# Splitting the late output-projection weights around the last keys and values, and moving the last group's transposes together

## The chip, the cores and the metric

The kernel runs on one core of a Trainium2 chip. The core has a matrix engine (PE, whose weight loads the profile lists as PEld), a vector engine (DVE), a scalar engine (ACT), a general engine (POOL) and SyncE (SP), which here issues all transfers. The metric is the device time of one execution in microseconds; smaller is better.

## The reference

One decoding step (one new token for each of four sequences) of a block: attention over a cached window and a gated feed-forward part, both modulated by a condition c. All data are 32-bit floats.

```python
mod = (silu(c) @ w_mod).reshape(4, 6, 1, 512)         # sa, ca, ga, sb, cb, gb
h = layernorm(x) * (1 + ca) + sa                       # x: 4 x 1 x 512
q = (h @ wq)                                           # 32 heads of 128
k, v = last 2048 rows of k_cache, v_cache              # 8 key heads, each shared by 4 query heads
a = softmax(q k^T / sqrt(128)) v @ wo                  # wo: 4096 x 512
x = x + ga * a
h = layernorm(x) * (1 + cb) + sb
x = x + gb * ((silu(h @ w1) * (h @ w3)) @ w2)          # w1, w3: 512 x 1792; w2: 1792 x 512
```

## The kernel before

**Memory and transfers.** Some 101 MB are read once, in the order in which they are used. They pass through one buffer, `ring`, of three slots; a slot has two halves of 8192 floats a partition. `load(dst, src, cuts)` issues on SP one transfer for each piece that `cuts` names. SP issues in program order, and an issue waits until the piece's old content has been used. The order is: modulation weights of the first part, x and c, wq, then the keys and values (K and V) of the eight groups of heads, 8 MB a group, in turn into the slots. Group g's load is written behind group g-3. Group 7's load is written behind group 5, in two pieces (K, then V) into slot 1. Ahead of it in the queue goes `wo_mod` into slot 0: the first half of wo (for groups 0 to 3) with the modulation weights of the second part. Behind group 7's go the second half of wo (4 MB, for groups 4 to 7) into the place of group 6's K, `w1` into that of group 6's V, then `w3` in two pieces and `w2` in five (6, 4, 2, 1 and 1 of its 14 chunks) into slot 0.

**A group (`group(g)`, line 310).** Scores: four tiles `s_ps[t]` of 512 keys each, four products (one for each sequence) into a tile, and a maximum `mx` on DVE. Then `heads_out(g - 1)` (line 303) turns the previous group's result `o_sb` into columns of `oT` with four products and a DVE copy. Then for each tile t: an exponential on ACT into `p_sb[t]`, four transposes on PE into one of two PSUM banks that alternate, a DVE copy to `pT[t]`, and, one tile behind, the products with V, which add up in `o_ps` over the four tiles. Last, ACT scales `o_ps` into `o_sb`.

**The projection (`project_out(g)`, line 294).** Four products of `oT[:, g]` with wo, added up in `a_ps` over the eight groups. Those of groups 0 to 3, and the modulation's columns `mod_b`, stand between groups 6 and 7 on PE; those of groups 4 to 6 stand behind group 7; then come `heads_out(7)` and the projection of group 7.

**The rest.** Lines 358 to 403 follow one upon another: copy of `a_ps`, a norm and modulation (`norm`, `modulate`, `transposed`, short steps on PE, DVE and ACT), `ffn_in` with w1 and with w3 (16 products each, over the four parts k of 512 in turn, then transposes), the 14 chunks of products with w2, two DVE operations and the store.

Each float product is shown in the profile as two MATMUL instructions, so a projection is 8 of them and a group's scores are 32. All operations are recorded through one helper, so that all have line 53 in the profile; tiles tell them apart. Waits are derived from the buffers that operations touch: the part of a load's target that is overwritten decides what SP waits for.

Of the kernel before, what the change touches and what calls it, by code (L numbers as in the profile page):

```python
# [8 lines left out]
B, D, HQ, G, SK, DH, W, FF = 4, 512, 32, 8, 8192, 128, 2048, 1792  # L9
P = 128  # L10
R = HQ // G
NT = 4
# [6 lines left out]
HALF = 8192  # L19
# [122 lines left out]
def block_kernel(nc, xc_in, w_mod_a, wq, kv_in, wo_mod, wo, w1, w3, w2, out):  # L142
# [5 lines left out]
    do = Program(nc)  # L148

    def sb(name, *shape):  # L150
        return nc.alloc_sbuf_tensor(name, (P, *shape), F32).ap()

    def ps(name):
        return nc.alloc_psum_tensor(name, (P, 512), F32).ap()

    ring = sb("ring", 6 * HALF)
    slots = [ring[:, n * 2 * HALF : (n + 1) * 2 * HALF] for n in range(3)]
    s_ps = [ps(f"s_ps{t}") for t in range(NT)]
    banks = [ps(f"bank{n}") for n in range(2)]
    a_ps, o_ps = ps("a_ps"), ps("o_ps")  # L160
    turn = [0]

    def bank():
        turn[0] += 1
        return banks[turn[0] % 2]

    def load(dst, src, cuts=(0, 1)):
        step = src.shape[1] // cuts[-1]
        for lo, hi in zip(cuts[:-1], cuts[1:]):
            do("sync", "dma_start", dst[:, lo * step : hi * step], src[:, lo * step : hi * step])  # L170
        return dst[:, : src.shape[1]]
# [13 lines left out]
    kv = [None] * G  # L185
# [28 lines left out]
    oT = sb("oT", G, R, B)  # L214
# [9 lines left out]
    ss, ln, r0, ve, a, r = (sb(n, 1) for n in ("ss", "ln", "r0", "ve", "a", "r"))  # L224
# [68 lines left out]

    def project_out(g):
        for i in range(R):
            do("tensor", "matmul", a_ps[32 * i : 32 * i + B, :], oT[:, g, i, :], wo_t[g // 4][:, g % 4, i, :], start=(g == 0), stop=(g == G - 1))

    mx, nm, ls, l, rl = (sb(n, m) for n, m in (("mx", NT), ("nm", 1), ("ls", NT), ("l", 1), ("rl", 1)))
    p_sb = [sb(f"p_sb{t}", 512) for t in range(NT)]
# [3 lines left out]
    def heads_out(g):  # L303

        otp = bank()[:, : R * B]
        for c in range(NC):
            do("tensor", "matmul", otp, o_sb[:, c * P : (c + 1) * P], pick[:, c].rearrange("p r b -> p (r b)"), start=(c == 0), stop=(c == NC - 1))
        do("vector", "tensor_copy", oT[:, g].rearrange("p r b -> p (r b)"), otp)

    def group(g):  # L310
        kt, vt = (kv[g][:, i * HALF : (i + 1) * HALF].rearrange("p (t b n) -> p t b n", t=NT, b=B) for i in range(2))
        for t in range(NT):
            for b in range(B):
                do("tensor", "matmul", s_ps[t][32 * b : 32 * b + 32, :], qT[:, g, b, :], kt[:, t, b, :], start=True, stop=True)
            do("vector", "reduce_max", mx[:, t : t + 1], s_ps[t], axis=AX.X)
        do("vector", "tensor_reduce", nm, mx, axis=AX.X, op=ALU.max, negate=True)
        if g:
            heads_out(g - 1)
        for t in range(NT):
            do("scalar", "activation", p_sb[t], s_ps[t], AF.Exp, bias=nm, accum_out=ls[:, t : t + 1])  # L320
            pt = bank()
            for c in range(NC):
                do("tensor", "transpose", pt[:, c * P : (c + 1) * P], p_sb[t][:, c * P : (c + 1) * P], ident)
            do("vector", "tensor_copy", pT[t], pt.rearrange("p (c b i) -> p b c i", b=B, i=32)[:, :, :, :R])
            for u in [t - 1] * (t > 0) + [t] * (t == NT - 1):
                for b in range(B):
                    do("tensor", "matmul", o_ps[32 * b : 32 * b + NC * R, :], pT[u][:, b].rearrange("p c r -> p (c r)"), vt[:, u, b, :], start=(u == 0), stop=(u == NT - 1))
        do("vector", "reduce_sum", l, ls, axis=AX.X)
        do("vector", "reciprocal", rl, l)
        do("scalar", "activation", o_sb, o_ps, AF.Copy, scale=rl)  # L330

    for g in range(G - 1):
        group(g)
        if g < 4:
            kv[g + 3] = load(slots[(g + 2) % 3], kv_in[g + 3])
        elif g == 4:
            wom = load(slots[0], wo_mod)
        elif g == 5:
            load(slots[1], kv_in[7], (0, 1, 2))
            kv[7] = slots[1]  # L340
    wo_t = [t.rearrange("p (g r n) -> p g r n", g=4, r=R) for t in (wom[:, :HALF], load(slots[2][:, :HALF], wo))]
    w1_t = load(slots[2][:, HALF:], w1)
    for g in range(4):
        project_out(g)
# [2 lines left out]
    ga, sh, cb1, gb = (mod_b[:, i * P : (i + 1) * P] for i in range(4))  # L347
    mod_columns(wom[:, HALF:].rearrange("p (k j i) -> p k j i", k=4, j=4), mod_b, 4)
    do("vector", "tensor_scalar_add", cb1, cb1, 1.0)
    group(G - 1)  # L350
    w3_t = load(slots[0][:, HALF:], w3, W3_CUTS)
    w2_t = load(slots[0][:, :HALF], w2, W2_CUTS)
    for g in range(4, G - 1):
        project_out(g)
    heads_out(G - 1)
    project_out(G - 1)

    do("scalar", "copy", work, a_ps)
# [49 lines left out]
def _layout(i):  # L408
    import numpy as np

    def a(t):
        return np.ascontiguousarray(t)

    k = i["A_k_cache"][:, :, SK - W :, :].reshape(B, G, NT, 512, DH)
    v = i["A_v_cache"][:, :, SK - W :, :].reshape(B, G, NT, NC, P, DH)
    wm = i["w_mod"].reshape(4, P, 6, 4, P)
    xc = np.zeros((4, 32, P + 16), np.float32)
    xc[:, ::8, :P] = i["A_x"].reshape(B, 4, P).transpose(1, 0, 2)
    xc = xc.reshape(P, P + 16)
    xc[:, P:] = i["c"].reshape(B, 4, P).transpose(2, 1, 0).reshape(P, 16)  # L420
    w2 = i["B_w2"].reshape(14, P, D)
    wo = a(i["A_wo"].reshape(2, 4, R, P, D).transpose(0, 3, 1, 2, 4)).reshape(2, P, 8192)
    return {
        "xc_in": xc,
        "w_mod_a": a(wm[:, :, :2].transpose(1, 0, 3, 2, 4)).reshape(P, 4096),
        "wq": a(i["A_wq"].reshape(4, P, G, 512).transpose(1, 2, 0, 3)).reshape(P, 16384),
        "kv_in": np.concatenate([k.transpose(1, 4, 2, 0, 3).reshape(G, P, 8192), v.transpose(1, 4, 2, 0, 3, 5).reshape(G, P, 8192)], 2),
        "wo_mod": np.concatenate([wo[0], a(wm[:, :, 2:].transpose(1, 0, 3, 2, 4)).reshape(P, 8192)], 1),
        "wo": wo[1],
        "w1": a(i["B_w1"].reshape(4, P, FF).transpose(1, 0, 2)).reshape(P, 4 * FF),  # L430
        "w3": a(i["B_w3"].reshape(4, P, FF).transpose(1, 0, 2)).reshape(P, 4 * FF),
        "w2": a(np.stack([w2[4 * j + c] for c, j in CHUNKS], 1)).reshape(P, NF * D),
    }
# [15 lines left out]
```

## Time and profile before

| | |
|---|---|
| Median of 3 runs | 244.43 us (244.31 to 244.51) |
| The profiled execution's own time | 243.92 us |
| Its span, first to last instruction | 242.5 us |
| Mean granted clock of PE | 0.866 of full speed |
| Read from memory | 101.26 MB, 418 GB/s over the span |
| Busy: PE, DVE, ACT, POOL | 147.2, 47.6, 33.4, 2.1 us |

A row of the timeline has the start and the length in us, the engine, the operation with what it writes and reads, the count of instructions merged into the row, and in brackets how long the engine had stood idle and what ended that. In the chain of waits each entry is a start, a length and what the time was spent in, each released by the one before it. In the rows of stretches, "PE busy (x)" is busy time with the number of instructions, and PEclk the granted clock. The load of q1 is the DMA queue that SP feeds.

### The profile page before, as it was taken

Reading aid. Unit: us, or ns where it says so; the run is one execution under the profiler, and the core shown is the slowest. Engines: PE = TensorE matmul, PEld = TensorE weight load, DVE = VectorE, ACT = ScalarE, POOL = GpSimd, SP = SyncE. Lnnn points to the kernel's source line nnn. Section 1 sums busy time; section 2 is a strip of 40 time slices with the busy share of each in tenths; the row PEclk is TensorE's granted clock in tenths of the full one; section 3 lists DMA queues with packets and bytes.
Section 4 is the critical chain, followed back from the end, with each engine's and each line's share of the span. In section 5 each row is a group of like instructions: output and inputs, shape, how many; then the busy total and the mean of one; then the engine's idle time right before and its main releaser. Section 6 shows DMA issues by size and latency. Waiting matters only on the chain.

```text
span 242.5 us, 2543 instructions
## 1 busy us (share of the span) xinstructions
PE 147.2 (61%) x1106; PEld 52.2 (22%) x1106; DVE 47.6 (20%) x155; ACT 33.4 (14%) x84; POOL 2.1 (1%) x9
## 2 busy tenths in 40 slices
PE   0260392088278558838819919838836885873975
PEld 0120121023014113204202302411411232121234
DVE  3230003042023014104105103203200150104021
ACT  2000000004104103103200310410410022101020
POOL 3000000000000000000000000000000000000000
PEclk9999999579859958979967985997995996798599
DMA  7997979898989898989898999999999999999992
GB/s 251 453 519 346 519 346 511 357 508 358 497 368 489 378 497 368 489 378 486 378 486 381 476 390 476 411 446 411 454 405 405 430 432 432 432 435 407 426 410 95
DMA packets 3322, 101.48 MB, mean 418 GB/s; under 512 B 368, under 2 KB 624, under 8 KB 1008
## 3 DMA queue, kind: packets, MB, share of 16 engines
q1 hardware_dynamic: 3312, 101.33, 97.4%
q8 instruction: 8, 0.13, 0.2%
q14 instruction: 2, 0.02, 0.0%
HBM read 101.26 MB, written 0.07 MB: 418 GB/s over the span
## 4 chain that ended last, share of the span: by engine, by line
DMA 74%; PE 21%; DVE 2%; ACT 1%; issue 1%; SPq 1%; DVEq 0%; ACTq 0%
DMA ring<-kv_in 56%; DMA ring<-wo 18%; PE s_ps L53 12%; PE bank L53 4%; PE o_ps L53 3%; PE a_ps L53 2%; ACT p_sb L53 1%; SPq L53 1%; DVE mx L53 0%; DVE sq L53 0%; DVE p_sb L53 0%; ACT work L53 0%; DVE h L53 0%; DVE x L53 0%; DVE xc L53 0%
## 5 line engine op out<-in xcount | busy, mean ns | idle before, releaser
L53 PE MATMUL s_ps<-ring,qT 128*32 128x512 f32 x256 | 43.0, 833 | 43.0 <-DMA ring<-kv_in 43.0
L53 DVE TENSOR_REDUCE mx<-s_ps 128x1 f32<-128x512 f32 x32 | 22.1, 692 | 75.6 <-PE s_ps L53 75.6
L53 ACT ACTIVATE p_sb<-s_ps,nm 128x512 f32<-128x512 f32 x32 | 21.6, 686 | 104.8 <-PE bank L53 88.0
L53 PE MATMUL o_ps<-ring,pT 128*16 128x512 f32 x256 | 33.8, 624 | 2.9 <-DMA ring<-kv_in 2.9
L53 PE MATMUL bank<-ident,p_sb 128*128 128x128 f32 (+1 forms) x136 | 22.6, 290 | 10.4 <-ACT p_sb L53 9.8
L53 PEld LDWEIGHTS s_ps<-ring,qT 128*32 128x32 f32 x256 | 9.8, 148 | 75.5 <-DMA ring<-kv_in 39.5
L53 PEld LDWEIGHTS bank<-ident,p_sb 128*128 128x128 f32 (+1 forms) x136 | 14.7, 144 | 30.8 <-ACT p_sb L53 14.9
L53 DVE COPY pT<-bank 128x64 f32<-128x64 f32 x32 | 7.2, 225 | 42.0 <-PE bank L53 42.0
L53 PE MATMUL s_ps<-ring,hT 128*32 128x512 f32 x64 | 8.5, 693 | 10.5 <-DMA ring<-wq 10.5
L53 PE MATMUL a_ps<-ring,oT 128*4 128x512 f32 x64 | 9.4, 730 | 8.5 <-DMA ring<-wo_mod 6.0
L53 ACT ACTIVATE o_sb<-o_ps,rl 128x512 f32<-128x512 f32 x8 | 5.5, 687 | 41.1 <-PE o_ps L53 41.1
L53 PE MATMUL s_ps<-ring,h2T 128*32 128x512 f32 (+1 forms) x64 | 9.8, 705 | 0.4 <-DVE h2T L53 0.4
L53 PEld LDWEIGHTS bank<-pick,o_sb 128*128 128x128 f32 x64 | 7.8, 191 | 6.8 <-issue 6.8
L53 PE MATMUL bank<-pick,o_sb 128*128 128x16 f32 x64 | 8.5, 265 | 0.0
L53 PEld LDWEIGHTS o_ps<-ring,pT 128*16 128x16 f32 x256 | 5.1, 96 | 12.1 <-issue 9.6
L53 PE MATMUL bank<-tot,avg 128*128 128x1 f32 x4 | 1.0, 311 | 10.8 <-DVE tot L53 10.1
L53 PE MATMUL bank<-ring,sc 128*32 128x256 f32 (+1 forms) x64 | 7.2, 612 | 0.0
L53 ACT ACTIVATION_READ_ACCUMULATOR p_sb<-s_ps,nm 128x1 f32 x32 | 6.5, 203 | 0.0
L53 DVE COPY qT<-bank 128x64 f32<-128x64 f32 x8 | 2.2, 276 | 19.6 <-PE bank L53 19.3
L53 PEld LDWEIGHTS s_ps<-ring,hT 128*32 128x32 f32 x64 | 2.4, 127 | 16.0 <-issue 16.0
L53 PEld LDWEIGHTS a_ps<-ring,oT 128*4 128x4 f32 x64 | 1.6, 96 | 15.5 <-DMA ring<-wo_mod 6.9
L53 ACT ACTIVATE work<-s_ps 128x512 f32<-128x512 f32 x2 | 1.2, 597 | 24.4 <-PE s_ps L53 21.0
(72 smaller groups left out, 42.8 us busy)
## 6 DMA issues: line engine op xcount, KB each, us to landing
ring<-kv_in SPq DMA_DIRECT2D x2, 4096.0 KB, 42.8
ring<-wo SPq DMA_DIRECT2D x1, 4096.0 KB, 43.2
ring<-w SPq DMA_DIRECT2D x1, 3584.0 KB, 43.6
ring<-w SPq DMA_DIRECT2D x2, 1792.0 KB, 35.8
ring<-w_mod_a SPq DMA_DIRECT2D x1, 2048.0 KB, 7.9
ring<-w SPq DMA_DIRECT2D x1, 1536.0 KB, 40.4
ring<-w SPq DMA_DIRECT2D x1, 1024.0 KB, 42.4
ring<-w SPq DMA_DIRECT2D x1, 512.0 KB, 43.2
```

The source lines that it names most:

```text
L53: op = Op(engine, lambda: getattr(getattr(self.nc, engine), method)(*args, **kw), [])
```

## The change

The second half of wo is loaded as two quarters of 2 MB, into the same place as before. The third quarter (groups 4 and 5) is issued ahead of the last K, the fourth (groups 6 and 7) behind the last V and ahead of w1. The issue of the last K and V is now written behind group 6, behind the third quarter's. `wo_t` becomes a list of eight pieces, one for each group. In group 7 the projections of groups 4 and 5 stand between `heads_out(6)` and the transposes; all four tiles' transposes stand ahead of the first product with V; and the projection of group 6 stands behind `heads_out(7)`.

```diff
 def project_out(g):
     for i in range(R):
-        do("tensor", "matmul", a_ps[32 * i : 32 * i + B, :], oT[:, g, i, :], wo_t[g // 4][:, g % 4, i, :], start=(g == 0), stop=(g == G - 1))
+        do("tensor", "matmul", a_ps[32 * i : 32 * i + B, :], oT[:, g, i, :], wo_t[g][:, i, :], start=(g == 0), stop=(g == G - 1))
...
-def group(g):
+def group(g, projected=()):
...
     if g:
         heads_out(g - 1)
+    for done in projected:
+        project_out(done)
     for t in range(NT):
...
-        for u in [t - 1] * (t > 0) + [t] * (t == NT - 1):
+        if g < G - 1:
+            ready = range(max(t - 1, 0), t if t < NT - 1 else NT)
+        else:
+            ready = range(NT) if t == NT - 1 else ()
+        for u in ready:
             for b in range(B):
                 do("tensor", "matmul", o_ps[...], pT[u][...], vt[:, u, b, :], ...)
...
-    elif g == 5:
-        load(slots[1], kv_in[7], (0, 1, 2))
-        kv[7] = slots[1]
-wo_t = [t.rearrange("p (g r n) -> p g r n", g=4, r=R) for t in (wom[:, :HALF], load(slots[2][:, :HALF], wo))]
+quarters = [load(slots[2][:, : HALF // 2], wo[0])]
+kv[7] = load(slots[1], kv_in[7], (0, 1, 2))
+quarters.append(load(slots[2][:, HALF // 2 : HALF], wo[1]))
+wo_t = [t[:, n * 2048 : (n + 1) * 2048].rearrange("p (r n) -> p r n", r=R) for t in (wom[:, : HALF // 2], wom[:, HALF // 2 : HALF], *quarters) for n in range(2)]
 w1_t = load(slots[2][:, HALF:], w1)
...
-group(G - 1)
+group(G - 1, [4, 5])
 w3_t = load(slots[0][:, HALF:], w3, W3_CUTS)
 w2_t = load(slots[0][:, :HALF], w2, W2_CUTS)
-for g in range(4, G - 1):
-    project_out(g)
 heads_out(G - 1)
+project_out(G - 2)
 project_out(G - 1)
...
-        "wo": wo[1],
+        "wo": a(wo[1].reshape(P, 2, 4096).transpose(1, 0, 2)),
```

## The prediction

> **What bounds the kernel now.** I read the page first, for what is full over the whole span.
>
> ```profile
> span 242.5 us, 2543 instructions
> ...
> q1 hardware_dynamic: 3312, 101.33, 97.4%
> ```
>
> One queue fed by SP carries 101.33 MB and keeps its 16 engines busy for 97.4% of 242.5 us. The change moves the same bytes, so only what follows the stream can change. That is in the last entries of the chain of waits (start, length, what):
>
> ```profile
> 170.01 43.25 DMA ring<-wo
> ...
> 213.31 2.76 PE a_ps L53 x24
> ...
> 217.32 1.09 PE a_ps L53 x8
> ...
> 224.12 6.26 PE s_ps L53 x20
> ...
> 231.66 3.64 PE s_ps L53 x20
> ...
> 236.93 3.31 PE s_ps L53 x112
> ```
>
> The end does not hang on the last transfer. It hangs on wo, landed at 213.26: projections of groups 4 to 6 (24 matmul instructions), group 7's heads, its projection (8), the norm, the w1 products at 224.12, the w3 products at 231.66 and the w2 products at 236.93, without a wait for a transfer after wo. The question is how far behind this chain the stream is. The next fence pairs SP's issues (start) with their times to landing (last column), for w1, for the second half of w3 and for the last piece of w2, and gives the first and last start of the 112 w2 matmuls:
>
> ```profile
> 178.22 15.88 SPq L53 DMA_DIRECT2D ring<-w  x4
> ring<-w SPq DMA_DIRECT2D x1, 3584.0 KB, 43.6
> 193.30 0.33 SPq L53 DMA_DIRECT2D ring<-w  x1
> ring<-w SPq DMA_DIRECT2D x1, 1792.0 KB, 37.1
> 195.57 7.38 SPq L53 DMA_DIRECT2D ring<-w  x1
> ring<-w SPq DMA_DIRECT2D x1, 256.0 KB, 43.5
> L53 PE MATMUL s_ps<-ring,hidT x112: 272/273/298, 236.9 to 239.9; 128*32 128x128 f32 x112
> ```
>
> w1 lands at 178.22 + 43.6 = 221.8, 2.3 us ahead of its first use; the second half of w3 at 230.4; the last chunk of w2 at 195.57 + 43.5 = 239.07. That chunk is matmuls 105 to 112: 104/111 of the 2.99 us from first to last start puts it at 239.73. So the stream is only 239.73 - 239.07 - 0.05 (landing to first matmul, as 213.26 to 213.31) = 0.61 us ahead of the chain. This is the ceiling of the change: however much the chain gains, behind the last landing come 242.5 - 239.73 = 2.77 us of last chunk, two DVE operations and the store.
>
> **The change part by part.** The terms come from the timeline (start, length, instruction, idle time before it) of groups 6 and 7:
>
> ```profile
> 164.84 5.11 PE L53 MATMUL s_ps<-ring,qT 128*32 128x512 f32 x32 [4.86 <-DMA ring<-kv_in]
> 169.87 1.06 PE L53 MATMUL bank<-pick,o_sb 128*128 128x16 f32 x8
> 173.00 0.69 ACT L53 ACTIVATE p_sb<-s_ps,nm 128x512 f32<-128x512 f32 x1
> 175.70 0.66 PE L53 MATMUL bank<-ident,p_sb 128*128 128x128 f32 x4
> 184.18 5.65 PE L53 MATMUL a_ps<-ring,oT 128*4 128x512 f32 x32 [5.98 <-DMA ring<-wo_mod]
> 193.88 3.64 PE L53 MATMUL s_ps<-ring,qT 128*32 128x512 f32 x32 [0.62 <-DMA ring<-kv_in]
> 203.68 1.91 PE L53 MATMUL o_ps<-ring,pT 128*16 128x512 f32 x8 [2.90 <-DMA ring<-kv_in]
> 209.16 1.91 PE L53 MATMUL o_ps<-ring,pT 128*16 128x512 f32 x16
> 211.14 0.69 ACT L53 ACTIVATE o_sb<-o_ps,rl 128x512 f32<-128x512 f32 x1 [9.79 <-PE o_ps L53]
> ```
>
> *The queue.* The third quarter is issued once group 6's first two score tiles are done (half of 5.11 us behind 164.84, and late because the clock is low there: about 168.3), and the last K and V wait behind it on SP, though their own buffer is free earlier. At 168.3 wo_mod is still in flight and lands at 184.18, so 16 us of transfer cover the later issue; I cost it at nothing. If that cover were gone, each us would delay everything behind. One more DMA (0.33 us on SP) is likewise covered. SP's last issue already stalls for 7.38 us with no harm, since nothing stands behind it until the store; with one more transfer outstanding it may stall until V lands, 30 us ahead of its landing at 239.07. Costed at zero.
>
> *Landings.* Between the waits that wo_mod and K ended lie 9.70 us for 4 MB, so a 2 MB quarter takes 4.85. The third lands near 189.0, K at 198.7 instead of 193.85, V at 208.5 instead of 203.65, the fourth at 213.3, where wo landed. All behind it stays put. The rows of a quarter are half as long (16 KB). w3, whose two halves have rows of 14 KB, was complete 230.4 - 221.8 = 8.6 us behind w1: 2 x 1792 KB at 427 GB/s, against 432 for K, which on 4 MB is 0.1 us. I take 0.05, and 0 to 0.15 for the range.
>
> *The clock ahead of K.* PE finishes the modulation's columns at 193.88 - 0.62 = 193.26 and now idles 5.4 us until K. Here are windows of 3.41 us that begin where the granted clock changes (us, PE busy, clock, DMA share, GB/s):
>
> ```profile
> 161.01:164.42 3.41, 0.00 (x0) 1.00 0.99 423
> 164.42:167.84 3.42, 3.00 (x16) 0.50 1.06 460
> 167.84:171.25 3.41, 3.10 (x28) 1.00 0.84 365
> 198.56:201.97 3.41, 1.26 (x8) 1.00 1.05 452
> 201.97:205.38 3.41, 1.70 (x8) 0.50 0.98 423
> 205.38:208.80 3.42, 3.42 (x18) 0.50 0.98 417
> 208.80:212.21 3.41, 2.27 (x20) 1.00 0.99 426
> 222.45:225.86 3.41, 2.22 (x15) 0.50 0.97 412
> 225.86:229.28 3.42, 3.42 (x23) 0.50 1.04 440
> ```
>
> A full-clock window with 0.00 or 1.26 us of work is followed by half clock. A half-clock window with 3.00 or more is followed by full clock; one with 1.70 or 2.22 is not. With the same windows, 195.14 to 198.56 is empty, so the clock falls at 198.56, and the scores, from 198.75, fill the next window as group 6's did. They take group 6's 5.11 rather than 3.64, plus 0.1 for the slightly longer half-clock part: ended at 203.95. The Trainium skill, "TensorE: Matmul & The Clock Gate", Part 1, says that an idle window of about 3.4 us halves the clock and a busy one restores it; the trace agrees (0.50 behind the window of 0.00 us, 1.00 behind those of 3.00 and 3.42), and this rule speaks against the change here. Without the rule the sum would have scores of 3.64 us and PE 1.5 us earlier, which the ceiling makes worth nothing.
>
> *Group 7.* Heads of group 6 end 1.0 later, 204.95. Projections 4 and 5, 16 instructions, take 16/24 of the 2.76 us that 24 took behind wo, 1.8, to 206.75. The first exponentials are ready by then; the last ends as in group 6, 173.69 - 164.84 = 8.85 behind the scores' start, 207.6 (plus 0.1). So the projections put off the transposes by about 0.9 us. Four tiles at 0.66: ended at 209.4, behind V's landing at 208.5. The products with V then run without a break, 2 x 1.91 = 3.8, to 213.2 (211.07 before). Copy of the result 0.07 + 0.69, heads 1.0: 215.0. Projection 6 (0.9) covers the heads' copy to oT, projection 7 takes 1.04: ended at about 217.0 against 218.36. The chain gains 1.35 us: of the 2.76 us of projections behind wo 0.9 stay, and the later K and V take back the rest of the difference.
>
> *Behind it.* The w1 products can start at 224.12 - 1.35 = 222.75, still 0.95 behind w1's landing. They fill the window from 222.45 for 3.1 us, so the clock rises at 225.86 instead of 229.28: by group 6's rate (3.00 us at half clock do what 1.53 us at full clock do) they end near 227.9 instead of 230.4. The w3 products follow 1.28 later as before, at 229.2, and need w3's second half 1.8 us in, at 231.0; it landed at 230.4. The w2 products start 5.27 behind those, as 236.93 behind 231.66, at 234.5. They now run into the pieces of w2, and the last one starts at 239.07 + 0.05. Even if the clock rose as late as before, 6.5 us at half clock and 0.3 at full clock would end the w1 products at 229.6, 0.8 us earlier than before, and 0.61 is needed.
>
> *Sum.* Ceiling 0.61; less 0.05 for the shorter rows, and 0.02 of a possible 0.25 for a clock that falls while PE waits for pieces of w2 (the last chunk takes 0.5 us to DVE and half as much again at half clock, if one window of about 1.9 us of work counts as idle; 1.70 did not raise it and 1.26 dropped it, so this is undecided, though the drop would mostly come too late). Gain 0.54 us: span 241.96. The profiled execution took 243.92 us, 1.42 beside its span, and the shown median, 244.43, lies 0.5 above it. Taken off the median: 243.89.
>
> **The rivals.** *The stream ends no differently, and the chain gains nothing.* The phase of the windows decides. Group 5 met its keys 1.5 us into a window, which did not fill, and its scores took longer:
>
> ```profile
> 145.48 6.24 PE L53 MATMUL s_ps<-ring,qT 128*32 128x512 f32 x32 [5.42 <-DMA ring<-kv_in]
> ```
>
> With 6.24 for 5.11 the gain of 1.35 falls to 0.2, and with it the whole gain: 244.2. For it: PE idles ahead of K for 5.4 us, as ahead of group 5. Against it: the boundary at 198.56 lies 0.2 us ahead of K's landing. The Trainium skill ("TensorE: Matmul & The Clock Gate", Part 1) says that the windows run free of the kernel's start; the three runs, within 0.2 us, do not look like it.
>
> *Slower: the transposes behind the projections.* If the window with the scores does not restore the clock at all before 205.38, the scores take 6.9, and heads, projections, transposes and V products follow one upon another, with V long landed: 198.75 + 6.9 + 1.0 + 1.8 + 2.64 + 3.8 = 214.9, then 3.75 us to the end of projection 7, 218.7, which is 0.35 later than before. With the half-clock part of the w1 products unimproved, 244.8; a little more if heads or projections run at half clock too. It decides from 1.35 us of extra work at half clock between K and the last product. For it: every wait there is gone, so nothing absorbs a delay. Against: group 6's row.
>
> *Faster than the ceiling.* The runs shown are 0.5 us longer than the profiled one. If that is PE at half clock and not the stream, the same last landing cuts off up to 1.1: 243.3. Nothing in the profile tells.
>
> *The change does nothing since the stream bounds already.* The 0.61 is exact to about 0.1 in this execution; an end set by the stream in the other runs would leave 244.4.
>
> **How the numbers follow.** A difference of about 0.2%, 0.49 us, is what measurement of this kernel can tell. The end on the last piece of w2 has 0.58, with a range of its own of 243.65 to 244.1; some two thirds of it lie below 243.94. Below the ceiling 0.10; the chain or the stream giving nothing 0.14 and 0.05; slower 0.13. So faster 0.38 + 0.10 = 0.48, same 0.20 + 0.19 = 0.39, slower 0.13. The range, 243.3 to 244.7, takes in the extra of the shown runs and stops short of the slower rival's end.
>
> **What the profile after would show.** K's wait ends near 198.7 and V is no longer waited for; granted clock 0.50 from 198.6 to 202; projections 4 and 5 (16 instructions) behind the heads of group 6; projection 7 ended near 217.0; the w1 products start near 222.7; and the chain ends on a transfer of w2 (239.1), not on wo. A last w2 landing later than 239.3, scores above 6 us, or a projection 7 ended after 217.9 would make the prediction wrong.

## The result and the profile after

The changed kernel took 243.40 us (the median of six runs, from 243.22 to 243.73), the kernel before, beside it, 245.02 (six runs, 244.31 to 245.98): a ratio of 0.9934, with a 95% interval of 0.9906 to 0.9961. Measured once more the ratio was 0.9945 (0.9921 to 0.9970). The profiled executions took 243.22 us against 243.92. So the gain is 0.70 us between the two profiles and 1.0 to 1.6 us between the medians measured side by side; that difference is the main thing to explain. Part of it is sampling: the kernel before spreads so widely that its median is 245.02 over these six runs, 244.41, 244.37 and 244.21 over 33, 35 and 17 later ones, and 243.90 over 17 more.

The page has the same stream and a shorter span:

```profile
span 241.9 us, 2545 instructions
...
q1 hardware_dynamic: 3456, 101.33, 97.6%
```

The end of the chain of waits no longer goes back to wo. It goes back to the last chunk of w2, landed at 239.14 as before:

```profile
198.17 40.97 DMA ring<-w
239.14 0.04 issue
239.18 0.47 PE s_ps L53 x8
...
240.00 0.29 DVE p_sb L53
```

PE's timeline of the last group and behind it:

```profile
198.78 5.11 PE L53 MATMUL s_ps<-ring,qT 128*32 128x512 f32 x32 [5.62 <-DMA ring<-kv_in]
...
204.81 1.90 PE L53 MATMUL a_ps<-ring,oT 128*4 128x512 f32 x16
206.64 2.07 PE L53 MATMUL bank<-ident,p_sb 128*128 128x128 f32 x16
208.63 3.62 PE L53 MATMUL o_ps<-ring,pT 128*16 128x512 f32 x32
...
214.06 1.90 PE L53 MATMUL a_ps<-ring,oT 128*4 128x512 f32 x16
...
221.98 5.44 PE L53 MATMUL s_ps<-ring,h2T 128*32 128x512 f32 x32 [0.45 <-DVE h2T L53]
...
234.25 1.52 PE L53 MATMUL s_ps<-ring,hidT 128*32 128x128 f32 x48 [0.50 <-DMA ring<-w]
236.66 1.08 PE L53 MATMUL s_ps<-ring,hidT 128*32 128x128 f32 x32 [0.89 <-DMA ring<-w]
...
239.18 0.43 PE L53 MATMUL s_ps<-ring,hidT 128*32 128x128 f32 x8 [0.20 <-DMA ring<-w]
```

K is waited for until 198.78 and V no longer; projections 4 and 5 fill the place ahead of the transposes; projections 6 and 7 end at 214.06 + 1.90 = 215.96, against 218.36 before. The w2 products begin at 234.25 instead of 236.93 and then wait for the pieces of w2 in turn. In the windows (us, PE busy, clock, DMA share, GB/s) the clock falls once ahead of K and once in the norm:

```profile
191.54:194.95 3.41, 1.61 (x16) 1.00 1.00 432
194.95:198.37 3.42, 0.00 (x0) 1.00 1.07 460
198.37:201.78 3.41, 3.00 (x16) 0.50 1.00 432
...
215.43:218.85 3.42, 1.34 (x18) 1.00 0.99 428
218.85:222.26 3.41, 1.34 (x7) 0.50 0.94 399
```

### The profile page after: what moved, and what is told of

Read it like the earlier page. It is cut to its first block, busy times and chain, and to the rows that moved or that the text cites. A ratio compares the mean times of both kernels' runs of the same rounds, so it can differ in the third digit from the quotient of the medians.

```text
span 241.9 us, 2545 instructions
## 1 busy us (share of the span) xinstructions
PE 145.0 (60%) x1106; PEld 52.0 (21%) x1106; DVE 47.6 (20%) x155; ACT 33.4 (14%) x84; POOL 2.1 (1%) x9
## 4 chain that ended last, share of the span: by engine, by line
DMA 73%; PE 19%; another core or an unknown queue 2%; SPq 2%; DVE 1%; ACT 1%; issue 1%; ACTq 0%
DMA ring<-kv_in 37%; DMA ring<-wo_mod 18%; DMA ring<-w 17%; PE s_ps L53 7%; PE o_ps L53 5%; PE bank L53 5%; SPq L53 2%; PE a_ps L53 2%; ACT p_sb L53 1%; DVE mx L53 1%; DVE p_sb L53 0%; DVE nm L53 0%; ACTq L119 0%
## 5 line engine op out<-in xcount | busy, mean ns | idle before, releaser
L53 PE MATMUL s_ps<-ring,qT 128*32 128x512 f32 x256 | 43.8, 847 | 48.6 <-DMA ring<-kv_in 48.6
L53 PE MATMUL o_ps<-ring,pT 128*16 128x512 f32 x256 | 31.7, 596 | 0.0
L53 PE MATMUL bank<-ident,p_sb 128*128 128x128 f32 (+1 forms) x136 | 21.4, 283 | 9.4 <-ACT p_sb L53 8.8
L53 PE MATMUL s_ps<-ring,h2T 128*32 128x512 f32 (+1 forms) x64 | 9.1, 662 | 0.5 <-DVE h2T L53 0.5
L53 PE MATMUL s_ps<-ring,hidT 128*32 128x128 f32 x112 | 4.1, 277 | 1.8 <-DMA ring<-w 1.8
## 6 DMA issues: line engine op xcount, KB each, us to landing
ring<-w SPq DMA_DIRECT2D x1, 3584.0 KB, 43.7
```

What stands on the lines that cost most here:

```text
L53: op = Op(engine, lambda: getattr(getattr(self.nc, engine), method)(*args, **kw), [])
```

## The experiments

**The kernel before, profiled again**, unchanged, to see what differs between its executions.

> A second look at the kernel before. Theory (its end is wo's landing plus a PE chain whose length hangs on where the clock's 3.41 us windows fall): wo lands within 0.2 us of 213.3 and w2's last chunk within 0.2 us of 239.1, while the w2 products start anywhere from 235.5 to 240, and the span follows their start. Rival (the stream differs from run to run): the landings move with the span.

> A third look at the kernel before, for the same two theories: landings fixed within 0.2 us and the start of the w2 products anywhere from 235.5 to 240 (theory), or landings that move with the span (rival).

The first of these took 244.34 us, the other 246.09. Spans: 242.9 and 244.7. Chain of waits of the longer one, then its last issue on SP with the time to landing, then four windows:

```profile
171.13 42.26 DMA ring<-wo
...
213.44 4.46 PE a_ps L53 x24
...
226.35 6.20 PE s_ps L53 x20
...
239.10 3.31 PE s_ps L53 x112
```

```profile
194.98 8.09 SPq L53 DMA_DIRECT2D ring<-w  x1
ring<-w SPq DMA_DIRECT2D x1, 256.0 KB, 44.2
```

```profile
210.92:214.34 3.42, 0.90 (x12) 1.00 1.00 429
214.34:217.75 3.41, 3.41 (x20) 0.50 1.02 437
217.75:221.17 3.42, 2.45 (x28) 1.00 0.92 394
221.17:224.58 3.41, 1.35 (x12) 0.50 1.04 441
```

wo lands at 213.39 and the last chunk of w2 at 239.18, both within 0.13 us of the execution shown in the prediction. But a window that ends at 214.34 caught PE's wait for wo with 0.90 us of work; the clock fell, and the 24 projection instructions took 4.46 us instead of 2.76. It fell again at 221.17, in the norm. The w2 products start at 239.10 instead of 236.93. In the 244.34 one the clock fell in the norm alone, at 219.49 where the execution shown before has 222.45, and they start at 237.34:

```profile
237.34 3.26 PE L53 MATMUL s_ps<-ring,hidT 128*32 128x128 f32 x112 [0.35 <-DVE hidT L53]
```

```profile
216.08:219.49 3.41, 2.42 (x24) 1.00 1.02 437
219.49:222.90 3.41, 1.17 (x4) 0.50 0.96 408
```

In these three executions the landings agree and PE's chain varies with the phase of the clock's windows, as the theory had it. The window boundaries (222.45 in the execution shown before, 214.34 here) lie 2.4 windows of 3.41 us apart, so their phase differs from execution to execution.

**The changed kernel again.**

> The changed kernel again, beside the runs of the kernel before. Theory (the changed kernel ends on the last landing of w2, the kernel before on a PE chain whose length hangs on where the granted clock falls): 243.2 to 243.7 us whatever the mean granted clock of a run, while the kernel before spreads by about 1 us or more over its runs. Rival (both end on PE, only 1.3 to 2 us apart): the changed kernel spreads as much as the kernel before.

243.43 us (243.20 to 243.58), beside 244.41 (243.44 to 246.22) for the kernel before. One spreads by 0.4 us, the other by 2.8: the theory held. In this execution the windows lay otherwise, the scores took 6.21 us and projection 7 ended 1.2 us later than in the profile above, and the span was still 242.0:

```profile
198.85 6.21 PE L53 MATMUL s_ps<-ring,qT 128*32 128x512 f32 x32 [6.19 <-DMA ring<-kv_in]
...
239.27 0.43 PE L53 MATMUL s_ps<-ring,hidT 128*32 128x128 f32 x8 [0.20 <-DMA ring<-w]
```

**The quarters and the early projections, without the transposes.**

```diff
-            if g < G - 1:
-                ready = range(max(t - 1, 0), t if t < NT - 1 else NT)
-            else:
-                ready = range(NT) if t == NT - 1 else ()
+            ready = range(max(t - 1, 0), t if t < NT - 1 else NT)
```

> The changed kernel with the last group's transposes back between its products with V; quarters and early projections stay. Theory (the stream bounds, PE has about 2.2 us to spare): the products with V end near 213.5 instead of 212.25, and the time is that of the changed kernel within 0.2 us. Rival (the order of the transposes is part of the gain): about 1.2 us more than the changed kernel, 244.6.

243.31 us (243.14 to 243.58), ratio 0.9949 (0.9927 to 0.9971). The products with V ended at 213.74, 1.5 us later than in the changed kernel, and that cost no time. In the profiled execution the w2 products just met the last landing (198.28 + 41.0 = 239.28), with PE's spare time used up:

```profile
211.83 1.91 PE L53 MATMUL o_ps<-ring,pT 128*16 128x512 f32 x16
...
236.31 3.42 PE L53 MATMUL s_ps<-ring,hidT 128*32 128x128 f32 x112 [0.35 <-DVE hidT L53]
```

**The transposes alone**, in the kernel before.

```diff
-            for u in [t - 1] * (t > 0) + [t] * (t == NT - 1):
+            for u in ([t - 1] * (t > 0) + [t] * (t == NT - 1) if g < G - 1 else range(NT) if t == NT - 1 else ()):
```

> The kernel before with only the last group's transposes moved ahead of all its products with V; wo in one piece, projections 4 to 6 behind it. Theory (the end hangs on wo's landing at 213.3 and on what is behind it): the products with V end near 207.5 instead of 211.1, PE waits longer for wo, no gain: within 0.5 us of the kernel before either way, since the emptier stretch ahead of wo may move the fall of the clock into the projections. Rival (the transposes carry the gain): 0.6 to 1.6 us less than the kernel before.

245.68 us (243.54 to 246.99), ratio 1.0035 (1.0000 to 1.0070). The products with V ended at 207.3, and in the profiled execution the longer wait for wo was a whole window without work; the 24 projection instructions behind it ran at half clock:

```profile
213.38 5.30 PE L53 MATMUL a_ps<-ring,oT 128*4 128x512 f32 x24 [6.08 <-DMA ring<-wo]
```

```profile
208.39:211.80 3.41, 0.00 (x0) 1.00 1.04 442
```

No gain, and probably a loss; the median lies 1.3 us above that of the kernel before, more than expected. Work done sooner ahead of a wait lengthens the wait.

**The loads alone**: quarters as in the change, the transposes in the old order, and the projections of groups 4 to 7 all behind `heads_out(7)` (in the kernel before, those of groups 4 to 6 stand ahead of it).

```diff
-    group(G - 1, [4, 5])
+    group(G - 1)
...
     heads_out(G - 1)
-    project_out(G - 2)
+    for g in range(4, G - 1):
+        project_out(g)
```

> Only the loads of the change: quarters as in the changed kernel, the transposes between the products with V as before, and the projections of groups 4 to 6 all behind the last group's heads. Theory (the gain is that projections leave the place behind wo, and the kernel before's longest runs are those where the clock falls in PE's wait ahead of wo): projection 7 ends near 218.9, 0.5 later than in the profiled execution of before, so the end hangs on PE again, at 243.6 to 244.6; but PE no longer waits for wo, so runs of 245 and more are gone. Rival (splitting the load alone carries the gain): 243.3 to 243.5, like the changed kernel.

244.89 us (243.30 to 246.54), ratio 1.0023 (0.9989 to 1.0057): no gain. The loads only make room; the gain needs the projections in it. Half of the expectation fell: the median lies above the range given, and runs above 245 are still there. PE does not wait for wo now, but it waits for V, and in the profiled execution the clock fell there, into the products with V:

```profile
208.83 1.64 PE L53 MATMUL o_ps<-ring,pT 128*16 128x512 f32 x8 [1.28 <-DMA ring<-kv_in]
...
217.26 3.62 PE L53 MATMUL a_ps<-ring,oT 128*4 128x512 f32 x32
```

```profile
205.73:209.15 3.42, 1.58 (x12) 1.00 0.89 378
209.15:212.56 3.41, 3.41 (x20) 0.50 1.11 468
```

Its order also leaves PE idle for 0.81 us while ACT scales the result; with projections 4 to 6 in their old place that time would be used. That variant was not run.

**The last chunk of w2 not loaded**, in both kernels.

```diff
-    w2_t = load(slots[0][:, :HALF], w2, W2_CUTS)
+    w2_t = load(slots[0][:, :HALF], w2[:, : (NF - 1) * 512], W2_CUTS[:-1])
```

> The changed kernel without the load of w2's last chunk (256 KB); the last eight matmuls use the chunk before it. Theory (the last landing sets the end): the end falls by the 0.63 us between the last two landings, to about 242.8. Rival (PE sets the end): no change.

> The kernel before without the load of w2's last chunk (256 KB); the last eight matmuls use the chunk before it. Theory (its end hangs on PE from wo's landing on, and the stream is ahead by 0.6 us or more): no change, within 0.2 us of the kernel before apart from its spread. Rival (the stream bounds the kernel before too): about 0.5 us less, as the same cut gave on the changed kernel (243.43 to 242.96).

The changed kernel fell to 242.96 us (242.85 to 243.15, no run as long as the shortest of the whole one); the kernel before stayed, 244.40 beside 244.37, ratio 1.0005 (0.9973 to 1.0037). That interval alone would not exclude a fall of 0.47 us (0.9981), but the profiled execution shows the kernel before without a wait for w2:

```profile
237.33 3.27 PE L53 MATMUL s_ps<-ring,hidT 128*32 128x128 f32 x112 [0.35 <-DVE hidT L53]
```

So the stream ends the changed kernel, and PE ended that execution of the other. The fall was 0.47 rather than 0.63, probably since 16 matmul instructions, not 8, stand behind the last landing of the shortened stream (194.97 + 43.7 = 238.7).

**PE kept busy in the norm of the kernel before.**

```diff
+def idle(n):
+    for _ in range(n):
+        do("tensor", "transpose", s_ps[3][:, :P], ident, ident)
...
 do("scalar", "copy", work, a_ps)
+idle(3)          # and 3, 3 and 6 more around the two matmuls of the norm
```

> The kernel before with 15 transposes of the identity (0.165 us each) into an unused PSUM tile, in PE's gaps of the second norm. Theory (the kernel before loses to the fall of the clock ahead of the w1 products): the w1 products take 3.6 to 4 us instead of 5 to 6.3, the end meets the stream in most runs, and the median falls by 0.5 to 1 us towards 243.4 to 243.8. Rival (the place of the projections counts, not the clock): no gain, or a loss of some 0.2 us for the added instructions.

243.46 us (243.11 to 244.40), ratio 0.9971 (0.9947 to 0.9996), with the loads and the projections where they were before. The w1 products run at full clock, and the end meets the stream:

```profile
224.08 3.63 PE L53 MATMUL s_ps<-ring,h2T 128*32 128x512 f32 x32 [0.38 <-DVE h2T L53]
...
239.20 0.42 PE L53 MATMUL s_ps<-ring,hidT 128*32 128x128 f32 x8 [0.20 <-DMA ring<-w]
```

Five of its twelve runs still lie between 244.1 and 244.4, and they are of two kinds. Three have spans of 242.9 to 243.1 us; these executions were not profiled, and that the clock fell ahead of wo in them is only likely. The other two have spans of 241.8 and 242.0, like the short runs, but 2.3 us beside the span instead of 1.3 to 1.5; what took that time is not shown.

**PE kept busy ahead of the last K**, in the changed kernel (`idle(28)` ahead of the last group).

> The changed kernel with 28 transposes of the identity (4.6 us) on PE in its idle time ahead of the last K. Theory (the half clock that the later K brings costs PE 1.5 us, which its spare time hides): the last group's scores take 3.6 us instead of 5 to 6.2, and the time stays at 243.3 to 243.5. Rival (the slow scores cost time): 0.5 us or more less.

243.44 us (243.03 to 244.73), ratio 0.9965 (0.9938 to 0.9992). The scores at full clock (3.64 us) gain nothing: PE then waits for V, and the w1 products wait for w1.

```profile
198.91 3.64 PE L53 MATMUL s_ps<-ring,qT 128*32 128x512 f32 x32 [1.76 <-DMA ring<-kv_in]
...
208.63 3.63 PE L53 MATMUL o_ps<-ring,pT 128*16 128x512 f32 x32 [1.25 <-DMA ring<-kv_in]
...
222.11 6.10 PE L53 MATMUL s_ps<-ring,h2T 128*32 128x512 f32 x32 [0.78 <-DMA ring<-w]
```

Four of its runs lie between 244.1 and 244.8, where the changed kernel has none. Two of them have spans of 241.9 and 242.0 and 2.2 and 2.6 us beside the span, as above; the others have spans of 242.9 and 243.4. Why stays open; for the longer spans the new wait for V is the place that I would look at.

**Three more projections behind the last**, in the changed kernel, into `s_ps[3]`.

```diff
+for _ in range(3):
+    for i in range(R):
+        do("tensor", "matmul", s_ps[3][32 * i : 32 * i + B, :], oT[:, G - 1, i, :], wo_t[G - 1][:, i, :], start=True, stop=True)
 do("scalar", "copy", work, a_ps)
```

> The changed kernel with three more projections (24 matmul instructions, 2.7 us) into an unused PSUM tile behind the last one, on PE's chain. Theory (PE has 1 to 2.3 us to spare, by where the clock falls): of the 2.7 us some 0.4 to 1.5 show, 243.8 to 244.9 with a spread over the runs like that of the kernel before. Rival (PE's chain sets the end of the changed kernel): 2.7 us more, 246.1.

243.48 us (243.21 to 244.20), ratio 0.9959 (0.9933 to 0.9986): the median did not move, less than expected. The ACT copy hides part of the 2.7 us, and the clock fell only at 225.17 (218.85 in the profile above). In the profiled execution PE's spare time was just used up: the chain of waits ends on PE, and the w2 products ended at 239.91, 0.8 us behind the last landing (198.23 + 40.9 = 239.1), where the changed kernel has 0.5:

```profile
217.25 2.76 PE L53 MATMUL s_ps<-ring,oT 128*4 128x512 f32 x24
...
224.69 5.33 PE L53 MATMUL s_ps<-ring,h2T 128*32 128x512 f32 x32 [0.38 <-DVE h2T L53]
...
236.65 3.26 PE L53 MATMUL s_ps<-ring,hidT 128*32 128x128 f32 x112 [0.35 <-DVE hidT L53]
```

**A smaller store**, an attempt to go below the changed kernel by its tail.

```diff
-    do("sync", "dma_start", out, res)
+    do("sync", "dma_start", out, res[::8])
```

> The changed kernel with a store of the 16 partitions that hold the result (8 KB) instead of all 128 (64 KB). Theory (the time is the last landing plus a fixed tail): what the store saves shows in full; of the 1.55 us from issue to landing some 0.4 are its 144 packets, so the median falls by 0.1 to 0.4 us, to 243.0 to 243.3. Rival (the store's time is all fixed): no change.

243.52 us (243.43 to 243.77), ratio 0.9957 (0.9929 to 0.9985): no gain. From issue to landing the 8 KB from every eighth partition took 1.7 us, the 64 KB of the changed kernel 1.5:

```profile
out<-p_sb SPq DMA_DIRECT2D x1, 8.0 KB, 1.7
```

## Why the prediction was right, and where its size was not

**The queue and the landings** came as worked out: third quarter 189.0, K 198.7, V 208.4, fourth quarter 213.3, last chunk of w2 239.14 (0.07 later than before, where 0.05 was taken for the shorter rows). The later issue of K and V delayed nothing.

**The clock ahead of K** fell as forecast (0.50 from 198.37 to 201.78) and the scores took 5.11 us. That the size matched was luck: the boundary lay by chance within 0.2 us of the 198.56 taken from the execution before, and in the next execution the scores took 6.21 us. Kept at full clock they saved no time, as the ceiling said.

**Group 7** was better than its sum. Two terms were too long: four tiles of transposes without products between them take 2.07 us rather than 4 x 0.66, and 32 instructions with V take 3.62 rather than 3.8. That is 0.8 of the 1.05 us by which the chain gained more than forecast, 2.4 us instead of 1.35. The w1 products now start 0.2 us behind w1's landing (178.11 + 43.7 = 221.81), which is the next bound: with PE kept busy ahead of K they waited for it, idle for 0.78 us instead of 0.38.

**The ceiling** was the step that decided, and in the profiled execution it was right: forecast span 241.96, measured 241.9; forecast gain 0.54, measured 0.70 between the profiled executions. It is shown by the chain's end on w2, by the cut stream that shortens the changed kernel, and by 1.5 us of later V products and three more projections that left the median where it was, though they used up PE's spare time in the profiled executions.

**What failed** is in "Taken off the median: 243.89". The 0.61 us by which the stream was ahead belongs to one execution, in which PE's chain was among the short ones. In the two others the stream is ahead by 1.0 and 2.7 us (w2 products at 237.34 and 239.10 instead of 236.93, landings within 0.13 us), and the change takes away all of that. So the median gained 1.0 to 1.6 us side by side, not 0.54, and the median 243.4 lies below the likeliest case's own range of 243.65 to 244.1. It is the rival "faster than the ceiling", to which I gave 0.10 and the time 243.3; the range held because its lower end was put there, not by the sum. I had set aside the reason for it because three runs lay within 0.2 us of each other; with 108 of them the kernel before spreads from 243.4 to 246.3, and 21 lie no higher than the longest of the changed kernel, 243.73. The Trainium skill's sentence that the windows run free ("TensorE: Matmul & The Clock Gate", Part 1) was right, and the trace agrees: the boundaries 222.45 and 214.34 above are not a whole number of windows apart.

**The slower rival** did not happen: the window with the scores restored the clock. In the execution where it did so a window later, with scores of 6.21 us, the time stayed at the stream's end as well. That is the condition of the rival "the chain gains nothing", and the prediction's own sign of being wrong (scores above 6 us); both had the price too high, since the chain has 2.4 us to give and not 1.35.

Of the change's three parts, the early projections carry the gain and the split load makes them possible; the transposes add 1.5 us to PE's spare time and nothing to the time.

## What to carry to other kernels

Where a stream of transfers and a chain on PE end close together, what one profile shows as their distance belongs to one phase of the clock: the gain of shortening the chain is the distance in the typical execution, so read several profiles before taking it off a median. The kernel that ends on its stream was also the steadier one here (0.4 us against 2.8). Move work out from behind the last wait; work moved ahead of it without being taken from behind it only lengthened the wait here, and dropped the clock for what followed.

## What the hardware showed that was not expected

PE's busy time in a window of 3.41 us does not by itself tell whether the clock falls. Full-clock windows with 0.00, 0.90, 1.34 and 1.58 us of work were followed by half clock and one with 1.61 was not; but the windows with 2.42 and 2.45 us in the two further executions of the kernel before were followed by half clock too. So the rows in the prediction give no threshold for the fall, and what decides stays open.

The kernel before, with landings that agree within 0.13 us, took 243.92, 244.34 and 246.09 us in its three profiled executions; what differs in them is PE's time at half clock. Over all its runs it spreads by 2.9 us, and where spans are listed it has 1.3 to 1.5 us beside the span in every run, so that the spread lies inside the span. That the phase of the windows makes it in the runs without a profile too is inferred.

SP's last issue took 7.1 to 8.1 us instead of 0.33 in these executions, with nine or ten earlier transfers not yet landed, at no cost here, as nothing stood behind it until the store. What held it is not shown.
